# Keys ahead of queries, value scaling in halves on ScalarE, a shorter scale chain and a new order in a fused attention and mixture-of-experts kernel

## The chip, the cores and the metric

The kernel runs on one core of a Trainium2 chip. The metric is the device time of one execution in microseconds (us); a kernel's time is the median of several runs. The core has TensorE (PE, matrix products into the accumulator memory PSUM; PEld is its weight load), VectorE (DVE), ScalarE (ACT), GpSimd (POOL) and SyncE (SP), which here issues the transfers.

## The reference

```python
# attention: batch 4 x 8 heads, 768 tokens, head size 48
k_n = k / (np.linalg.norm(k, axis=-1, keepdims=True) + 1e-06)
for t in range(S):
    y[:, :, t] = np.einsum('bhd,bhde->bhe', q[:, :, t], state)
    v_old = np.einsum('bhde,bhd->bhe', state, kt)
    state = state + bt[:, :, :, None] * np.einsum('bhd,bhe->bhde', kt, vt - v_old)
# mixture of experts: 4 x 768 tokens of 384, 8 experts of width 1024
for s in range(S):
    fresh_e = int(np.argmax(logits[b, s]))
    e = fresh_e if s == 0 or local_gate[b, s] < 0.5 else prev_e
    ...
    out[b, s] = p[e] * (np.maximum(x[b, s] @ w1[e], 0.0) @ w2[e])
```

The attention output y is the input x of the experts. The state depends on the token before, so the kernel works in chunks of tokens: inside a chunk a triangular system replaces the steps one by one.

## The kernel before

**Chunks and macros.** 768 tokens are 12 chunks n of 64 tokens (all 32 heads at once); two chunks make one macro m = n // 2. For a chunk, `K(n)` loads its keys and queries (two tiles `W`, 512 KB each), takes the products of keys with keys and with queries (the Gram matrix, 48 matmuls per tile) into PSUM, and copies three parts out: the key products within each 32 tokens into `gt` (ACT L199 writes it, DVE L204 adds its other part), the cross part into `G2` (ACT L201), the query products under a mask into `am` (DVE L202). `T_(m)` transposes `gt` into L (DVE L212, two halves), and makes the scales: sum of squares `ss` (L214), its root (ACT L215), then seven small DVE operations (L216, L218, L220), the start value (`Diag`, L225) and the scaled system L (L226, L227). nT (L222) holds the key norms by which values are scaled.

**The solve.** Each macro's triangular system is solved in steps of two instructions. Macro 0 uses blocks of 16 (15 steps, L244 and L245), the others blocks of 32 (31 steps, L240 and L241). Macro 2 runs on DVE in PSUM, the other five on POOL; they are called S0, S1, S3, S4, S5 here. A macro's solution X is transposed (L253, L256), and `Tc(n)` builds from it the chunk's operand `XT`.

**Values and state.** Each chunk's values arrive in `kv` (768 KB); L313 multiplies them by nT, on DVE for eight chunks and POOL for four. `online(n)` then carries the state: matmuls fk and fq (keys and queries with the state), R (L325), p1 with XT, Us (ACT L339), the new state (ACT L346), p2, and the output y of the chunk (ACT L352, DVE L353). Below, O6 is this part for chunk 6 and U6 the query and y part of it. y goes to HBM (xs) and comes back transposed for the routing products (L362, L365).

**Experts.** After ten chunks a first share of tokens is routed, gathered and run through the experts while the last chunks still work; the rest follows.

**What sets the order.** All operations are numbered when the program is built, and the string ORDER lists the numbers with an engine letter (S, P, V, A, G, I). Every engine executes its operations in that order and waits in front of one whose inputs or buffers aren't ready. Buffers come from pools: 14 `W` tiles, three `kv`, three PSUM accumulators `pr`, two `gt`. An operation that may run on one of several engines (L313: `e='VG'`) runs on the one that ORDER names.

Of the kernel before, what the change touches and what calls it, by code (L numbers as in the profile page):

```python
# [70 lines left out]
class Attn:  # L71
# [4 lines left out]
    ORDER='''11S 7G 199S 8G 12S 24S 25S 79S 0G 2G 14P 9G 19P 15A 16A 18V 17V 26P 22V 21A 31P 67S 27A 29V 13S 20A 66S 30V 32A 4S 23V 99A 80S 35V 181S 36V 37V 74P  # L76
38V 39A 44A 40V 41V 28A 76A 69P 42V 75A 68S 45V 46V 153S 211S 77V 47G 198S 71A 43V 48G 210S 70A 78V 197S 72V 81P 49G 73V 50G 34V 10V 86P 51G 82A 83A
52G 85V 87A 53G 84V 88A 33A 90V 54G 92V 55G 91V 56G 89V 217P 182V 93V 57G 94A 212P 220V 219A 218A 154G 3V 221V 205P 213A 58G 95V 96V 59G 200P 97V 207A
60G 1A 215V 448S 206A 61G 280S 202A 216V 322S 214A 100V 101V 5S 201A 63V 103G 104G 62V 105G 64V 138P 106G 209V 107G 208V 139A 65V 108G 204V 140P 109G
223V 110G 222V 102V 111G 203V 224V 225A 230A 226V 112G 98V 227V 166P 281G 228V 142V 324S 113G 141V 231V 167A 233V 147A 168P 232V 114G 234V 235V 236V  # L80
115G 6V 237V 116G 238V 144P 169V 117G 239V 240V 145A 118G 170V 146P 241V 119G 172P 151A 150A 242V 149A 243V 152A 120G 148A 143A 244V 171A 155P 121G
245V 178A 173A 246V 175A 122G 174P 156A 247V 355A 157P 123G 248V 179A 249V 176A 159P 124G 306S 177A 323S 180A 250V 158A 125G 251V 183P 160A 252V 126G
229V 161V 127G 253V 185P 163S 128G 184V 336S 129G 254V 186P 335S 130G 255V 256V 131G 187A 257V 132G 190P 133G 258V 134V 188P 191A 135V 164P 404S 300A
165V 270A 192V 330P 136V 193S 342P 331A 194S 332A 334V 303A 333V 343A 405G 345V 344A 337P 296A 346V 274A 137V 325P 307G 338A 340V 326A 341V 339A 328V
327A 271P 329V 272A 195P 347V 277A 273P 189A 348V 349V 196V 350A 279A 351V 297P 276A 352V 275A 298A 353V 278A 299P 572S 357V 162S 356V 282P 358V 304A
301A 359G 259V 305A 302A 360G 260V 284P 283V 361G 362G 261V 262V 285P 446S 363G 263V 447S 264V 364G 286A 479A 287P 365G 289P 265A 430S 366G 288A 267V
367G 290A 308P 291V 368G 449P 354V 293S 309V 369G 310P 266V 570S 269V 370G 311P 460S 452V 584S 371G 312A 394A 315P 372G 401A 313P 316A 431V 294P 451A
373G 268V 420A 450A 317V 459S 374G 528S 295V 454P 319S 453V 375G 466P 455A 424A 458V 457V 398A 376G 461P 469V 456A 467A 377G 395P 378G 462A 396A 529V
468A 397P 427A 379G 470V 314A 465V 471V 421P 402A 380G 399A 403A 472V 463A 381G 473V 464V 474A 422A 400A 475V 320P 382G 423P 321V 476V 383G 406P 425A
428A 477V 384G 429A 480V 482V 408P 385G 407V 481V 409P 571S 386G 292S 387G 410A 388G 411P 389G 483G 390V 413P 652S 412A 583S 484G 426A 391V 414A 432P  # L90
485G 393V 548A 486G 392V 487G 415V 519P 488G 433V 417S 434P 520A 489G 518A 490G 435P 668S 491G 318S 521P 436A 492G 493G 437P 523A 522A 418P 554S 524A
# [905 lines left out]
```

## Time and the profile before

| | |
|---|---|
| three runs | 486.12, 486.02, 483.58 us; median 486.02 us |
| profiled execution | 483.22 us, of which the profile's span is 481.4 us |
| busy share of the span | PE 80%, DVE 69%, POOL 54%, ACT 39% |

The profile's execution has 1.8 us around its span. Times inside the trace count from the span's start. A row of a timeline gives start, length, engine, line, operation, output and inputs, and in brackets how long the engine was idle before and what ended that. A busy share is a mean over stages with different limits, so the rows that count are those of the stage in question.

### The profile page before, as it was taken

The numbers are of one execution on the slowest core, as the hardware profiler recorded it, in microseconds if no ns is written. First come the engines' busy times: TensorE is split into PE (matmuls) and PEld (weight loads), VectorE is DVE, ScalarE is ACT, GpSimd is POOL, SyncE is SP. The second block draws the span as 40 slices with busy tenths as digits, with TensorE's granted clock in tenths as the row PEclk, the third lists the DMA queues.
The fourth block names the chain that finished last, engine by engine and source line by source line (L and its number), as shares of the span: only waits on it lengthen the run. The fifth ranks groups of instructions, "written<-read, shape, count | busy, mean of one in ns | idle before, by whom it ended". The sixth has DMA issues, their size and how long they took to land. (4 is left out here: it accounts for less than half of the span.)

```text
span 481.4 us, 20215 instructions
## 1 busy us (share of the span) xinstructions
PE 383.2 (80%) x8907; PEld 291.6 (61%) x8907; DVE 333.3 (69%) x705; ACT 189.9 (39%) x340; POOL 260.7 (54%) x438
## 2 busy tenths in 40 slices
PE   5545676676775657685869999999999999999994
PEld 4535575575775656574658768675655656566662
DVE  1999877846661848689426878578787995958551
ACT  2531263643635354633645204225234251625120
POOL 5388881288878858986512353864251424351301
PEclk9795557777689777557679999999999999999999
DMA  8632037458165656518533235767665657585301
GB/s 294 258 132 98 4 114 204 68 177 275 39 199 170 127 156 154 157 35 210 189 101 76 59 106 180 163 130 260 183 203 145 192 180 226 160 269 163 92 1 48
DMA packets 61691, 72.19 MB, mean 150 GB/s; under 512 B 40172, under 2 KB 51534, under 8 KB 61600
## 3 DMA queue, kind: packets, MB, share of 16 engines
q1 hardware_dynamic: 58048, 60.90, 44.4%
q0 software_dynamic: 3552, 9.96, 6.3%
q8 instruction: 71, 1.16, 1.0%
q14 instruction: 20, 0.16, 0.1%
HBM read 52.53 MB, written 9.95 MB: 130 GB/s over the span
## 5 line engine op out<-in xcount | busy, mean ns | idle before, releaser
L241 POOL TENSOR_TENSOR X<-X,fg 128x31 f32<-128x31 f32 (+15 forms) x124 | 74.3, 600 | 9.7
L240 POOL TENSOR_TENSOR fg<-L,X 128x31 f32<-128x31 f32 (+15 forms) x124 | 64.9, 523 | 24.3 <-DVE X L225 8.3
L487 DVE TENSOR_SCALAR gf<-pr 128x384 f32<-128x384 f32 (+5 forms) x68 | 33.5, 495 | 26.5 <-PE pr L485 12.7
L154 PE MATMUL pr<-W 64*64 64x64 f32 (+1 forms) x1152 | 34.4, 281 | 21.7 <-DMA W<-in_kq_dram 7.6
L154 PE MATMUL pr<-S,W 64*64 64x48 f32 x1408 | 37.5, 274 | 14.6 <-issue 10.5
L154 PEld LDWEIGHTS pr<-S,W 64*64 64x64 f32 x1408 | 34.7, 189 | 19.1 <-issue 13.4
L154 PEld LDWEIGHTS pr<-W 64*64 64x64 f32 x1152 | 31.6, 168 | 24.1 <-issue 9.1
L485 PE MATMUL pr<-kv,xtp 128*128 128x384 f16 (+3 forms) x186 | 43.7, 298 | 0.8 <-ACT W L486 0.8
L492 PEld LDWEIGHTS <-W 128*128 128x128 f16 x288 | 27.7, 98 | 19.1 <-POOL W L699 1.4
L485 PEld LDWEIGHTS <-W 128*128 128x128 f16 x288 | 27.8, 99 | 17.6 <-issue 0.7
L485 PE MATMUL pr<-kv,W 128*128 128x448 f16 (+2 forms) x144 | 37.8, 341 | 0.0
L486 ACT ACTIVATE L<-pr 128x384 f16<-128x384 f32 (+3 forms) x34 | 15.2, 447 | 53.7 <-PE pr L485 23.6
L475 POOL DMA_INDIRECT out_dram<-y,so x9 | 11.2, 1249 | 45.8 <-DVE y L502 44.9
L485 PE MATMUL pr<-kv,amp 128*128 128x448 f16 (+3 forms) x120 | 34.4, 311 | 0.0
L486 ACT ACTIVATE W<-pr 128x256 f16<-128x256 f32 (+4 forms) x34 | 14.8, 441 | 46.0 <-PE pr L485 40.4
L473 POOL DMA_INDIRECT G<-xs,gi x23 | 26.0, 1129 | 7.0 <-issue 6.4
L470 DVE SCALAR_TENSOR_TENSOR W<-W,W 128x768 f16<-128x768 f32 (+1 forms) x23 | 26.3, 1143 | 3.2 <-ACT W L468 3.2
L154 PE MATMUL pr<-Us,amp 64*64 64x48 f32 x768 | 18.8, 251 | 12.0 <-issue 8.7
L492 PE MATMUL pr<-amp,L 128*128 128x384 f16 x116 | 28.3, 326 | 0.0
L492 PEld LDWEIGHTS <-L 128*128 128x128 f16 (+1 forms) x208 | 20.7, 101 | 12.2 <-issue 0.2
L492 PE MATMUL pr<-W,W 128*128 128x384 f16 x156 | 27.2, 326 | 0.0
L485 PEld LDWEIGHTS <-xtp 128*128 128x128 f16 x216 | 21.1, 98 | 9.5
(364 smaller groups left out, 979.5 us busy)
## 6 DMA issues: line engine op xcount, KB each, us to landing
W<-in_kq_dram SPq DMA_DIRECT2D x24, 512.0 KB, 5.5
W<-in_moe_w_dram SPq DMA_DIRECT2D x30, 384.0 KB, 3.4
W<-in_moe_w_dram SPq DMA_DIRECT2D x22, 512.0 KB, 4.4
kv<-in_kv_dram SPq DMA_DIRECT2D x12, 768.0 KB, 4.7
...
amp<-in_moe_w_dram SPq DMA_DIRECT2D x2, 512.0 KB, 6.7
...
```

Of the source, the lines that this page charges most:

```text
L154: mm=lambda o,l,r,st,sp,tp:MM(o,l,r,start=st,stop=sp,skip_group_check=True,tile_position=tp)
L240: eng.tensor_tensor(tv,l[:,j,j+1:].unsqueeze(2).to_broadcast([128,n,k]),x[:,j,0:k].unsqueeze(1).to_broadcast([128,n,k]),op=ALU.mult)
L241: eng.tensor_tensor(x[:,j+1:,0:k],x[:,j+1:,0:k],tv,op=ALU.subtract)
L470: def wlo(s,st,w,k): s.nc.vector.scalar_tensor_tensor(s.wv(w,k)[:,1],s.wst(st,k),256.0,s.wv(w,k)[:,0],op0=ALU.mult,op1=ALU.subtract)
L473: return s.nc.gpsimd.indirect_dma_start(out=x[0:m],out_offset=None,in_=s.xs[0:nt,:],in_offset=bass.IndirectOffsetOnAxis(ap=ix[0:m],axis=0) ...
L475: I=s.nc.gpsimd.indirect_dma_start(out=s.out[:,:],out_offset=bass.IndirectOffsetOnAxis(ap=ix[0:m],axis=0),in_=y[0:m],in_offset=None,bounds ...
L485: for k in range(3): s.nc.tensor.matmul(ps,s.wv(W[k],k)[:,a,0,128*f:128*f+128],xT[:,3*b+k,:],start=(x==0 and k==0),stop=(x==2 and k==2))
L486: def uphi(s,h,ps): s.nc.scalar.activation(h,ps,AF.Relu,scale=2.0**-6)
L487: def upt(s,t,ps): s.nc.vector.tensor_scalar(t,ps,0.0,2.0**-6,op0=ALU.max,op1=ALU.mult)
L492: s.nc.tensor.matmul(po[0:m],h(a,f)[:,c:c+m],s.wv(W[k],k)[:,b,f%2,:],start=(x==0 and f==0),stop=(x==2 and f==7))
```

## The change

1. For chunks 0 and 1 the host stores each key-and-query tile with the keys first. The program loads the key half of a tile (128x512) in one transfer and the query half in another, and forms the Gram products in two halves of 16 matmuls: the key half feeds `gt` and `G2`, the query half `am`. Each half takes a PSUM accumulator of its own.
2. The value scaling of a chunk is two operations of eight heads each, 24 in all. ORDER puts 21 on ACT (eight 128x48 instructions each, the scale a column of nT), two on POOL and one on DVE.
3. The addition of the other part into `gt` may run on ACT, as two copies of 32 partitions. ORDER does so for 10 of the 24 tiles.
4. The scale chain: behind the root stand three DVE operations in front of the scaled L; nT and what leads to it are operations of their own. L is scaled in a part of 8 columns and one of 24 (before two of 16), and a solve of blocks of 32 waits for the first part only until its eighth step.
5. ORDER is another order of all operations (1133 against 1107).

The experts' code, the pools' sizes and the engine of each solve stay.

```diff
-    ORDER='''11S 7G 199S 8G 12S 24S 25S 79S 0G 2G 14P 9G 19P 15A 16A 18V 17V 26P 22V 21A 31P 67S 27A 29V 13S 20A 66S 30V 32A 4S 23V 99A 80S 35V 181S 36V 37V 74P
...
+    ORDER='''11S 2G 12S 28S 29S 7G 109A 14P 8G 17S 53A 24S 30P 13S 15A 40S 9G 16A 20V 5S 21P 32A 33S 31A 210S 18P 36V 22A 25P 19V 76S 75S 27V 37P 88S 26V 89S 38A
...
+                if n<2:
+                    add(lambda g=g:nc.sync.dma_start(KQ[g].t.rearrange("r a t -> r (a t)")[:,0:512],s.kq_[n,g][:,0:512]),w=[(KQ[g],0)],claim=[KQ[g]],e='S',c=262144); s.kl[n]=S.ops[-1]
...
+                def fh(z,ps,g=g):
+                    k=KV(KQ[g].t,n)
+                    for u in range(4):
+                        for j,c,q in H:
+                            w=0 if u%2==0 else 1-z; y,d=q^w,c^w; mm(ps.t[B(y),d,128*u+64*z:128*u+64*z+64],k[B(j),u,q,0,:],k[B(j),u,q,z,:],u==0,True,(64*j,64*y))
...
+                def gh(e,go=go,gv=gv):
+                    if e is nc.vector: e.scalar_tensor_tensor(go(),gv()[:,:,:,32:64],s.ma[:,1:2],go(),op0=ALU.mult,op1=ALU.add)
+                    else:
+                        for q in range(2): o=slice(64*q+32,64*q+64); e.copy(go()[o],gv()[o,:,:,32:64])
...
-                add(lambda go=go,gv=gv:nc.vector.scalar_tensor_tensor(go(),gv()[:,:,:,32:64],s.ma[:,1:2],go(),op0=ALU.mult,op1=ALU.add),r=[ps,"mask",key],p=[gt],claim=[gt],c=485)
+                add(gh,r=[ps0,"mask",key],p=[gt],claim=[gt],e='VA',c=dict(V=485,A=760))
...
-            def f2():
-                nc.vector.tensor_mul(t0.t,t0.t,ss.t); nc.vector.tensor_add(t0.t,t0.t,s0.t); nc.vector.tensor_scalar(nn.t,t0.t,0.5,1e-6,op0=ALU.mult,op1=ALU.add); nc.vector.reciprocal(mu.t,nn.t)
...
-            def f3(): nc.vector.tensor_mul(t0.t,mu.t,b.t); nc.vector.tensor_mul(mu.t,mu.t,t0.t)
...
+            add(lambda:nc.vector.tensor_scalar_add(nn.t,ss.t,1e-12),r=[ss],w=[(nn,0)],claim=[nn],c=190)
...
+            def f2(): nc.vector.scalar_tensor_tensor(mu.t,s0.t,2e-6,nn.t,op0=ALU.mult,op1=ALU.add); nc.vector.reciprocal(mu.t,mu.t); nc.vector.tensor_mul(mu.t,mu.t,b.t)
...
-                add(fm,r=[(L,j//16)],w=[(Z,0),("fm",E_)],claim=[L,Z],e=EE,c=520+3.8*ne if EE=='G' else 400+2.15*ne); S.ops[-1].lock=not ps
+                add(fm,r=[(L,j//8 and 1)],w=[(Z,0),("fm",E_)],claim=[L,Z],e=EE,c=520+3.8*ne if EE=='G' else 400+2.15*ne); S.ops[-1].lock=not ps
...
-            add(lambda e:e.tensor_tensor(v(),v(),nT.t[:,16*cc:16*cc+16].unsqueeze(2).to_broadcast([128,16,48]),op=ALU.mult),r=[nT],w=[(kv,1)],claim=[kv],e='VG',c=dict(V=1050,G=1550)); S.ops[-1].pre.add(S.ops[-2]); S.ops[-1].lock=1
...
+            for h in range(2):
+                def sv(e,h=h):
+                    a=v()[:,8*h:8*h+8]; t=16*cc+8*h
+                    if e is nc.scalar:
+                        for x in range(8): e.mul(a[:,x],a[:,x],nT.t[:,t+x:t+x+1])
+                    else: e.tensor_tensor(a,a,nT.t[:,t:t+8].unsqueeze(2).to_broadcast([128,8,48]),op=ALU.mult)
```

**The first transfers.** SP's queue at the start of the program, before; W0 and W1 are the tiles of chunk 0, W2 and W3 those of chunk 1, bt the betas.

```order
L182 DMA W0_77<-in_kq_dram 128x1024
L185 DMA bt0_103<-in_beta_dram 128x32
L182 DMA W1_78<-in_kq_dram 128x1024
L182 DMA W2_79<-in_kq_dram 128x1024
L182 DMA W3_80<-in_kq_dram 128x1024
L182 DMA W4_81<-in_kq_dram 128x1024
```

The same place now:

```order
L185 DMA W0_77<-in_kq_dram 128x512
L185 DMA W1_78<-in_kq_dram 128x512
L185 DMA W2_79<-in_kq_dram 128x512
L185 DMA W3_80<-in_kq_dram 128x512
L217 DMA W0_77<-in_kq_dram 128x512
L217 DMA W1_78<-in_kq_dram 128x512
L189 DMA bt0_103<-in_beta_dram 128x32
L217 DMA W3_80<-in_kq_dram 128x512
```

The four key halves now stand ahead of every query half.

**The first scale chain.** DVE's queue from the transpose of `gt` to the scaled system of macro 0, before; s00 is the root, mm0 the scale, X1 the solution's tile.

```order
L212 STREAM_TRANSPOSE L0_120<-gt_112 128x512 x2
L214 TENSOR_SCALAR ss0_109<-L0_120 128x32
L216 RECIPROCAL t00_111<-s00_110 128x32
L218 TENSOR_TENSOR t00_111<-t00_111,ss0_109 128x32
L218 TENSOR_TENSOR t00_111<-t00_111,s00_110 128x32
L218 TENSOR_SCALAR nn0_105<-t00_111 128x32
L218 RECIPROCAL mm0_108<-nn0_105 128x32
L220 TENSOR_TENSOR t00_111<-mm0_108,bt1_104 128x32
L220 TENSOR_TENSOR mm0_108<-mm0_108,t00_111 128x32
L225 COPY X1_123<-mm0_108 128x32
L227 TENSOR_TENSOR L0_120<-L0_120,mm0_108 128x2x16x16
```

The same place now:

```order
L231 STREAM_TRANSPOSE L0_120<-gt_112 128x512 x2
L233 TENSOR_SCALAR ss0_109<-L0_120 128x32
L234 TENSOR_SCALAR nn0_105<-ss0_109 128x32
L236 SCALAR_TENSOR_TENSOR mm0_108<-s00_110,nn0_105 128x32
L236 RECIPROCAL mm0_108<-mm0_108 128x32
L236 TENSOR_TENSOR mm0_108<-mm0_108,bt0_103 128x32
L247 TENSOR_TENSOR L0_120<-L0_120,mm0_108 128x2x16x16
L245 COPY X1_123<-mm0_108 128x32
```

Seven operations between root and scaling became three, and the start value moved behind the scaling.

**ScalarE around the first operands.** ACT's queue before, where chunk 0's operand xtp0 is built and chunk 0 and 1 leave PSUM (QQ0, Q10: copies of products; Us0: L339).

```order
L267 COPY Q10_129<-pr1_148 128x512
L307 COPY xtp0_97<-TT0_124 32x16x32
L295 COPY QQ0_130<-pr0_147 128x256
L308 ACTIVATE xtp0_97<-pr0_147 32x2x4x32
L307 COPY xtp0_97<-TT0_124 32x16x32
L308 ACTIVATE xtp0_97<-pr0_147 32x2x4x32 x3
```

The same place now:

```order
L338 ACTIVATE kv2_102<-kv2_102,nT1_107 128x48 x8
L338 ACTIVATE kv1_101<-kv1_101,nT0_106 128x48 x8
L315 COPY QQ0_130<-pr0_147 128x256
L287 COPY Q10_129<-pr2_149 128x512
L328 ACTIVATE xtp0_97<-pr0_147 32x2x4x32 x3
L306 ACTIVATE xtp0_97<-TT0_124,ma_76 128x16x32
L327 COPY xtp0_97<-TT0_124 32x16x32
L338 ACTIVATE kv2_102<-kv2_102,nT1_107 128x48 x8
```

Groups of eight value scalings now stand between the copies that empty PSUM.

## Rows read from the trace of the kernel before

**Rows 1.** Page, busy time of engines: us, share of the span, instructions.

```profile
PE 383.2 (80%) x8907; PEld 291.6 (61%) x8907; DVE 333.3 (69%) x705; ACT 189.9 (39%) x340; POOL 260.7 (54%) x438
```

**Rows 2.** Windows: length, busy us of PE, PEld, DVE, ACT, POOL; PE clock; DMA share; GB/s.

```profile
35.37:74.30 38.93, 24.59 (x1185) 22.91 (x1186) 34.49 (x78) 13.22 (x24) 34.21 (x63) 0.51 0.25 78
...
95.75:134.40 38.65, 27.78 (x1216) 25.73 (x1211) 23.24 (x49) 18.15 (x36) 33.85 (x62) 0.72 0.50 157
...
179.20:222.50 43.30, 30.74 (x1209) 28.62 (x1210) 35.03 (x76) 19.36 (x31) 38.47 (x62) 0.65 0.54 144
...
265.00:481.40 216.40, 207.98 (x1646) 131.89 (x1643) 154.59 (x323) 69.31 (x116) 82.24 (x76) 1.00 0.53 153
```

**Rows 3.** POOL's waits: waited for, us in total, times, longest.

```profile
POOL fg L244 <- DVE L L227: 10.5, 1, 10.5
```

**Rows 4.** POOL's timeline: the starts of S1, S3 and S4.

```profile
35.37 0.24 POOL L240 TENSOR_TENSOR fg<-L,X 128x31 f32<-128x31 f32 x1 [0.69 <-DVE L L226]
...
95.75 0.51 POOL L240 TENSOR_TENSOR fg<-L,X 128x31 f32<-128x31 f32 x1 [8.29 <-DVE X L225]
...
135.75 0.24 POOL L240 TENSOR_TENSOR fg<-L,X 128x31 f32<-128x31 f32 x1 [1.37 <-DVE L L226]
```

**Rows 5.** POOL's timeline: start of S5, first gather behind S5.

```profile
179.20 0.24 POOL L240 TENSOR_TENSOR fg<-L,X 128x31 f32<-128x31 f32 x1 [4.58 <-ACT xtp L308]
...
225.18 1.27 POOL L473 DMA_INDIRECT hz<-xs,gi  x1 [2.73 <-DVE gi L669]
```

**Rows 6.** PE's timeline at the start.

```profile
4.20 1.98 PE L154 MATMUL pr<-W 64*64 64x128 f32 x48 [4.20 <-DMA W<-in_kq_dram]
7.85 5.04 PE L154 MATMUL pr<-W 64*64 64x128 f32 x144 [1.67 <-DMA W<-in_kq_dram]
```

**Rows 7.** Transfers of 0 to 8 us: packets, bytes, rate.

```profile
DMA packets 653, 1.90 MB, mean 237 GB/s; under 512 B 194, under 2 KB 194, under 8 KB 653
```

**Rows 8.** Transfer issued first: KB, us to landing.

```profile
W<-in_kq_dram SPq DMA_DIRECT2D x1, 512.0 KB, 3.3
```

**Rows 9.** ACT's timeline at the start.

```profile
6.30 1.28 ACT L199 ACT_TABLE_LOAD   x1 [6.30 <-PE pr L154]
...
12.97 0.47 ACT L199 ACTIVATE gt<-pr,ma 128x256 f32<-128x256 f32 x1 [0.52 <-PE pr L154]
```

**Rows 10.** DVE's timeline at the start.

```profile
14.02 1.99 DVE L212 STREAM_TRANSPOSE L<-gt 128x512 f32<-128x512 f32 x2
...
16.53 0.35 DVE L216 RECIPROCAL t<-s 128x32 f32<-128x32 f32 x1 [0.29 <-ACT s L215]
...
18.58 0.68 DVE L227 TENSOR_TENSOR L<-L,mm 128x512 f32<-128x512 f32 x1
```

**Rows 11.** Groups of ACT by shape: xcount, busy us, mean ns, idle before.

```profile
L308 ACT ACTIVATE xtp<-pr 32x256 f32<-32x256 f32 x48 | 17.3, 372 | 10.7 <-PE pr L154 10.2
...
L215 ACT ACTIVATE s<-ss 128x32 f32<-128x32 f32 x6 | 1.4, 230 | 11.6 <-DVE ss L214 11.5
```

**Rows 12.** Groups of DVE by shape, the same columns.

```profile
L204 DVE SCALAR_TENSOR_TENSOR gt<-pr,ma,gt 128x256 f32<-128x256 f32 x8 | 3.6, 478 | 13.9 <-ACT G L201 9.9 <-ACT gt L199 3.9
```

**Rows 13.** Line L313, value scaling: duration ns minimum/median/maximum.

```profile
L313 DVE TENSOR_TENSOR kv<-kv,nT x8: 895/950/1373, 28.0 to 238.5; 128x768 f32<-128x768 f32 x8
...
L313 POOL TENSOR_TENSOR kv<-kv,nT x4: 1472/1474/1477, 30.1 to 86.0; 128x768 f32<-128x768 f32 x4
```

**Rows 14.** DVE's timeline from S0's end to S3's start.

```profile
35.15 1.90 DVE L253 STREAM_TRANSPOSE TT<-X 128x512 f32<-128x512 f32 x2
```

**Rows 15.** PE's timeline in the same stretch.

```profile
74.13 1.21 PE L154 MATMUL pr<-S,W 64*64 64x48 f32 x36 [1.99 <-issue]
```

**Rows 16.** DVE's timeline ahead of S5.

```profile
176.75 0.96 DVE L353 SCALAR_TENSOR_TENSOR y<-pr,y 128x768 f16<-128x768 f32 x1 [5.09 <-ACT y L352]
177.70 1.23 DVE L470 SCALAR_TENSOR_TENSOR W<-W,W 128x1024 f16<-128x1024 f32 x1
...
178.93 0.17 DVE L365 TENSOR_SCALAR lg<-pr 128x18 f32<-128x18 f32 x1
```

More of the change, by code (lines that the diff above doesn't have):

```diff
@@ L79 @@
[L79 to L82, printed above, removed]
@@ L225, in T_, with fL @@
             add(lambda e:e.tensor_copy(zt()[:,0:1024:33],mu.t),r=[mu],w=[(Z,0),(Z,1)],claim=[Z],e='V',c=300)
-            def fL(e,z): l=full(L.t)[:,16*z:16*z+16]; e.tensor_mul(l,l,mu.t.unsqueeze(1).to_broadcast([128,16,32]))
+            def fL(e,z): a,b_=((0,8),(8,32))[z]; l=full(L.t)[:,a:b_]; e.tensor_mul(l,l,mu.t.unsqueeze(1).to_broadcast([128,b_-a,32]))
             def fl(e): l=blk(L.t); e.tensor_mul(l,l,mu.t.rearrange("p (z b) -> p z b",z=2).unsqueeze(2).to_broadcast([128,2,16,16]))
             if Bk==32:
-                for z in range(2): add(lambda e,z=z:fL(e,z),r=[mu,ss],w=[(L,z)],claim=[L],e='V',c=670); S.ops[-1].lock=1
+                for y in range(2): add(lambda e,z=y:fL(e,z),r=[mu,ss],w=[(L,y)],claim=[L],e='V',c=(400,1030)[y]); S.ops[-1].lock=1
             else: add(fl,r=[mu,ss],w=[(L,0),(L,1)],claim=[L],e='V',c=670); S.ops[-1].lock=1
             if ps:
-                for o in S.ops[i1-8-s.TS:]: o.boost=12e4
+                for o in S.ops[i1-9-s.TS:]: o.boost=12e4
             S.tag=('S',m)
@@ L323, in fk @@
                         for j,c,q in H: y,d=q^u%2,c^u%2; mm(pk.t[B(y),d,e48(u)],k(j,q,u,0),S0.t[B(j),q,u,:],u==0,True,(64*j,64*y))
[L324 to L325 removed]
+                add(fk,r=[*KQ,*((x,z) for x in KQ for z in range(2)),S0],w=[pk],e='P',c=1500); S.ops[-1].pc=(1800,1130,3.07,64); S.ops[-1].pre.update(C['xt']); ok=S.ops[-1]
+                add(lambda:nc.vector.tensor_tensor(R.t,kv.t[:,1].rearrange("p (c x) -> p c x",c=2),pk.t[:,:,0:384],op=ALU.subtract),r=[pk,(kv,1,0),(kv,1,1)],w=[R],claim=[kv],c=cv(768)+40)
                 S.tag=('U',n)
@@ L329, in fq @@
                         for j,c,q in H: mm(py.t[B(c),j,e48(u)],k(j,q,u,1),S0.t[B(j),q,u,:],u==0,False,(64*j,64*c))
-                add(fq,r=[*KQ,S0],w=[py],e='P',c=1500); S.ops[-1].pc=(1800,1130,3.07,64); S.ops[-1].pre.update([ok]+([ch[n-3]['lf']] if n>2 else [])); oq=S.ops[-1]; S.tag=('O',n)
-                rv=lambda q,c,u:R.t[B(q),c,e48(u)]; Rk=R
-            else: rv=lambda q,c,u:kv.t[B(q),1,384*c+48*u:384*c+48*u+48]; Rk=(kv,1)
+                add(fq,r=[*KQ,*((x,z) for x in KQ for z in range(2)),S0],w=[py],e='P',c=1500); S.ops[-1].pc=(1800,1130,3.07,64); S.ops[-1].pre.update([ok]+([ch[n-3]['lf']] if n>2 else [])); oq=S.ops[-1]; S.tag=('O',n)
+                rv=lambda q,c,u:R.t[B(q),c,e48(u)]; Rk=[R]
+            else: rv=lambda q,c,u:kv.t[B(q),1,384*c+48*u:384*c+48*u+48]; Rk=[(kv,1,0),(kv,1,1)]
             def p1():
```

109 lines of the change are left out of this document (62 added, 47 removed).

## The prediction, made before the changed kernel was run

> **What bounds the kernel now.** I read the page's busy shares first, then the windows by stage, then POOL's waits and timeline, then the timelines of the engines that POOL waits for. The busy shares [rows 1] name TensorE, but they are a mean. In the windows [rows 2] PE is dense only behind 265 us: 207.98 of 216.40 us, at a granted clock of 1.00. Before that no engine is full. So the end is the moment at which the dense part begins, plus some 216 us that the change does not touch; what the change is worth is how much earlier the attention gets there.
>
> Ahead of it the work is a relay. POOL solves S0, S1, S3, S4, S5 one after another, and its waits and timeline show the places where the relay stands still. It begins S0 at 19.45 (the edge of my first window; it waited 10.5 us for the scaled L [rows 3]), S1 at 35.37 after 0.69, S3 at 95.75 after a long gap, S4 at 135.75 after 1.37 [rows 4], S5 at 179.20 after 4.58 [rows 5]. So three starts carry the sum: S0 (limited by loads and a DVE chain), S3 (DVE and PE, while DVE also solves macro 2) and S5 (the chain of state and outputs).
>
> **The head.** Before, PE does the first tile's 48 matmuls at 4.20 (1.98 us) and then waits for a transfer until 7.85; the other 144 take 5.04 [rows 6]. By 8 us 1.90 MB have moved, 237 GB/s over the window [rows 7], and one 512 KB load issued into an empty queue takes 3.3 us to land [rows 8]. Four full tiles are 2.1 MB; the four key halves are half of that. At the same mean they are in by 8/1.9 × 1.05 = 4.4 us; by issue, since PE's first start at 4.20 puts the first issue at about 0.9, and with 1.3 us that I allow for three more, by 2.2 + 3.3 = 5.5. I take 5.3. A half is 16 matmuls, 0.6 us by the row of 144. It needs a third accumulator's release by one `am` or `gt` (0.5 to 0.7 each), so I put the last key half at 7.4 to 8.1. Its `gt` costs 0.47 on ACT [rows 9] and 0.48 on DVE [rows 12], or two copies of 0.37 on ACT [rows 11]. ACT's first table load, 1.28 us, stands on the path at 6.30 [rows 9]; in the new order it stands with two zero fills ahead of the first product, where ACT has nothing to do until about 4.9. So `gt` is full at about 9.5 and the DVE transposes begin at 9.6 instead of 14.02 [rows 10]. Bounds: 8.3 if ACT never waits (behind 4.9 stand four `gt` of 0.47, two `G2` and two copies of 0.37: 3.4 us), 11.5 if the fourth half queues behind a query half.
>
> The chain behind: the transposes take 1.99, the root comes back 0.52 after them (16.53 against 16.01), then seven operations take 2.05 up to L227 at 18.58, L227 0.68 [rows 10]. Three operations of 0.35, 0.2 and 0.2 are 0.8 with their pitches. So from 9.6: +2.0 +0.5 +0.8 +0.7 +0.2 for the start value behind it +0.2 to POOL = 14.0. I add 0.6 for waits that I can't see: **S0 at 14.6, 4.85 earlier** (3 to 6). S0 itself sheds the 1.47 scaling that stood inside it [rows 13]; the two-instruction steps stay. S0's end: 4.85 + 1.47 = 6.3 earlier.
>
> **From S0 to S3.** DVE begins S0's transposes at 35.15; S3 starts at 95.75 [rows 4, 14]. The 60.6 us between are a chain through DVE (macro 2's scale chain and its solve, the outputs) and PE (the state's products of chunk 1, still at 74.13 [rows 15], and then the Gram products of chunks 6 and 7). In it the change removes four DVE operations from macro 2's chain and four from macro 3's, 1.2 us each by the head's count, and moves three `gt` additions of 0.48 off DVE [rows 12]: 2.4 + 1.4 = 3.8. It adds on ACT five scaling halves and three pairs of copies.
>
> The price of a scaling half isn't in the trace: eight ACT instructions of 128x48. The nearest rows are 230 ns for 128x32 and 372 for 32x256 [rows 11], so 1.84 to 2.98 us a half; I take 1.95, near the first since 48 columns are near 32. DVE paid 0.95/2, POOL 1.474/2 a half [rows 13]. So 21 halves put 41 us on ACT, and ten pairs of copies 7.4: 190 us become 238 of some 470, half of the span. The rows leave the room: in the stretch from 35.37 ACT is 13.2 of 38.9 busy, in S3's 18.15 of 38.65 [rows 2].
>
> The Trainium skill, "ScalarE: Activation LUTs", section "Rules for kernel authors", says to do multiplications on VectorE and not on ScalarE, and so speaks against this part; from the instruction costs of the same page (186 ns + 0.833 ns an element, 93 more for the scale operand, overlapping by 93) I get an estimate of 1.9 us a half, so its sum would be the same. What would follow from it as an outcome is the rival of a late ACT below.
>
> Some halves stand ahead of copies that empty PSUM. Of five halves I count half a half each on average as 1.0 us in all on the path (0 if each falls into ACT's idle time, 9.8 if all are on it). So S3: 6.3 + 3.8 − 1.0 = **9.1 earlier, at 86.6** (85 to 90). PE's stall of 1.99 that nothing in the profile explains [rows 15] may move or vanish; I leave it.
>
> **S3 to S5.** S3 and S4 keep their steps. The wait of 1.37 ahead of S4 [rows 4] shrinks, since the solve starts when 8 columns of L are scaled: up to 1.2 back, but S4's end isn't what S5 waits for. S5 waits for its start value, which stands on DVE behind U6's output: that began at 176.75 after 5.09 us of waiting for ACT, then a weight conversion of 1.23 stood between [rows 16]. The trace names ACT xtp as S5's releaser, but nothing in S5's first step reads xtp, and the start value stands between the rows of 177.70 and 178.93; I take that. In the new order the conversion is gone from between, and two routing operations (0.18 each) and the small part of L (0.35) stand there: 0.5 less. The U6 chain begins in S3's stretch and shifts with it; six halves and one pair of copies (12.5 us) join ACT there, 18.15 + 12.5 of 38.65 = 79%. The four chunks' scalings gone from DVE return 0.95 each where DVE was in demand; I set that against ACT's delays. **S5 9.6 earlier.** S5 took 43.3 us, S3 38.65 for the same 62 instructions [rows 2]; less DVE work beside it may return up to 1 us. Behind S5, POOL now converts weights ahead of the gathers (which stood at 225.18 [rows 5]), and PE takes chunks 10 and 11 ahead of the first expert: between −4 and +2, for which I put 0.3 of loss against the 1 us.
>
> **Sum.** 9.6 + 1 − 0.3 = 10.3. The profiled execution took 483.22, of which 1.8 lies around the span: 472.9. The median of the three runs is 2.8 above it: 475.7. I say 474.0, between them; alone, this case has 470 to 479.
>
> **Rivals.**
>
> *ACT is late, no faster or slower.* ACT works in order; between S3's start and U6 stand nine halves, 17.6 us by my price, 26.8 by the upper one. Each that stands ahead of a copy of the state or of Us with PE waiting lengthens the chain to S5 by its whole 1.95. At 5 of 9 on the path, 10 us, the gain is gone (483 to 486); at all nine 490. For it: 79% in S3's stretch, and PE idles there often. Against it: PE's and ACT's idle times alternate in these stretches, and a half has a whole chunk's time, some 20 us, before R needs it. Chance 0.18, of which 0.11 is slower by over 0.5%.
>
> *Only the head gains.* S3 could be held by something not moved, as the key load of chunk 7 or the stall on PE, so that S1 and S2 move and S3 by the head alone, and part is lost again before S5: 5 us, 479 to 481. For it: the long gap ahead of S3 while POOL idles; against it: the gap's releasers are all DVE and PE operations that shift with S0. Chance 0.10.
>
> *The halves land no sooner.* If a load's time is mostly fixed and all share the same engines, the last key half lands with the bulk behind it, at about 7.5: the head gains only its chain and the table load, 2 us less than I say for S0 and for all that follows, and more if the query halves crowd in: 477 to 481. By rows: one load alone took 3.3 us for 512 KB, which at the later rate would be a good part fixed. Chance 0.05. The Trainium skill, "DMA: Bandwidth & Descriptors", section "Rules for kernel authors", wants 1 MiB a transfer, and would point to this; the trace has no 256 KB load to test it.
>
> *More.* If S5's wait of 4.58 falls with the chain (U6's output was late by the wait for ACT, 5.09) and the tail keeps its interleaving, 4 to 6 us more: 465 to 470. Chance 0.17.
>
> **Chances and range.** The forecast has 0.50. About 0.5% is what a measurement of this kernel can tell from no change. Faster by more: 0.50 + 0.17 + 0.10 + 0.05 = 0.82; within it 0.07 and slower 0.11, both from a late ACT. The range goes from 465 to 482; it leaves out the late ACT and a little of the low end. What I can't price is PE's clock: 0.51 in the stretch from 35.37 against 0.72 and 1.00 later [rows 2], near its lower level of 1.2 GHz; another spacing of matmuls may change it.
>
> **What would show it.** S0 starts at 14 to 15.5 with the transposes at 9 to 10.5; a scaling half is 1.8 to 2.1 us on ACT; S3 starts at 85 to 88; S5 at 168 to 171; behind 265 less about 10 PE is as dense as before. Wrong: transposes behind 12 (loads or accumulators); S3 behind 90 with DVE waiting for ACT (scaling in the way); U6's output later than 83 us after S3's start.

## The result and the profile after

The changed kernel is slower: 490.4 us against 485.0 on the same chip (20 runs each), ratio 1.0142 [1.0103, 1.0180]. Two more comparisons, in later groups of runs, gave 1.0102 [1.0033, 1.0172] and 1.0079 [1.0047, 1.0111]. A group of runs stands on one chip, and the groups differ (in six of them the kernel before had medians from 481.7 to 494.1 us). So a ratio is always to the kernel before on the same chip, and kernels are compared within a group where they can be. Two profiles of one kernel differ by up to 6 us at a stage, too: a single stage time says little, the same sign in several profiles says something. 474.0 us (465 to 482) had been predicted.

The page of the changed kernel, busy time of each engine, answers to [rows 1]; the profiled execution took 491.16 us, its span 489.4.

```profile
PE 388.2 (79%) x8971; PEld 297.2 (61%) x8971; DVE 323.4 (66%) x688; ACT 235.6 (48%) x532; POOL 260.2 (53%) x440
```

DVE lost 9.9 us and ACT gained 45.7, as planned. PE gained 5.0 of busy time and 64 matmuls.

POOL's timeline of the changed kernel: the starts of S0, S3, S4 and S5 and the first gather (L500).

```profile
19.79 0.24 POOL L264 TENSOR_TENSOR fg<-L,X 128x30 f32<-128x30 f32 x1 [10.87 <-DVE X L245]
...
95.45 0.24 POOL L260 TENSOR_TENSOR fg<-L,X 128x31 f32<-128x31 f32 x1 [23.65 <-DVE L L246]
...
138.93 0.24 POOL L260 TENSOR_TENSOR fg<-L,X 128x31 f32<-128x31 f32 x1 [6.19 <-DVE X L245]
...
180.01 1.04 POOL L260 TENSOR_TENSOR fg<-L,X 128x31 f32<-128x31 f32 x1 [3.68 <-DVE X L245]
...
228.79 1.47 POOL L544 TENSOR_TENSOR W<-W,c 128x768 f32<-128x768 f32 x1 [8.10 <-ACT W L495]
230.34 1.66 POOL L544 TENSOR_TENSOR W<-W,W 128x768 f16<-128x768 f32 x1
231.94 0.83 POOL L339 TENSOR_TENSOR kv<-kv,nT 128x384 f32<-128x384 f32 x1
233.29 1.26 POOL L500 DMA_INDIRECT hz<-xs,gi  x1 [0.51 <-DVE tq L698]
```

Against [rows 3 to 5]: S0 0.3 later, S3 0.3 earlier, S4 3.2 later, S5 0.8 later, the first gather 8.1 later, the end of the span 8.0 later. In this profile none of the three starts that carry the sum came more than 0.3 earlier; S1, at 33.19, was 2.2 earlier, and that was gone by S3. Two later profiles of the changed kernel, from other groups, have S0 at 19.64 and 20.13, S3 at 93.31 and 94.38 and S5 at 176.76 and 175.85. There S5 is 2.4 and 3.4 earlier than in the profile of before, and the kernel is slower all the same (1.0102 and 1.0079).

**The head.** PE's timeline at the start, against [rows 6], then DVE's, against [rows 10]:

```profile
4.45 1.13 PE L156 MATMUL pr<-W 64*64 64x64 f32 x32 [4.45 <-DMA W<-in_kq_dram]
5.87 1.98 PE L156 MATMUL pr<-W 64*64 64x64 f32 x64 [0.28 <-DMA W<-in_kq_dram]
8.55 3.80 PE L156 MATMUL pr<-W 64*64 64x64 f32 x125 [0.70 <-DMA W<-in_kq_dram]
14.46 0.33 PE L156 MATMUL pr<-W 64*64 64x64 f32 x3 [2.10 <-issue]
```

```profile
14.82 0.69 DVE L221 TENSOR_TENSOR amp<-pr,mask 128x512 f32<-128x512 f32 x1 [3.40 <-PE pr L156]
15.43 1.99 DVE L231 STREAM_TRANSPOSE L<-gt 128x512 f32<-128x512 f32 x2
...
17.96 0.19 DVE L236 SCALAR_TENSOR_TENSOR mm<-s,nn 128x32 f32<-128x32 f32 x1
18.19 0.35 DVE L236 RECIPROCAL mm<-mm 128x32 f32<-128x32 f32 x1
18.58 0.19 DVE L236 TENSOR_TENSOR mm<-mm,bt 128x32 f32<-128x32 f32 x1
18.80 0.69 DVE L247 TENSOR_TENSOR L<-L,mm 128x512 f32<-128x512 f32 x1
```

A half is 32 matmuls in the trace and takes 1.13 us. The text ahead of the prediction says 16: that is the program's count, and a product of f32 operands leaves two matmuls here; two halves are 64 where a whole tile was 48. The products of halves run on to 14.79 on PE. Three key halves are done at 7.85; then PE waits until 8.55 for a query half, and the last key half stands behind two query halves (its products take from 10.49 to 11.62). So `gt` was full at 12.94. On DVE an `am` (L221, which writes amp) stands ahead of the transposes and waited 3.40 us for a query half, 2.10 of it a stall of PE that the profile calls "issue" (no wait that it shows). The transposes begin at 15.43 instead of 14.02. The short chain behind them is as costed: 0.84 from 17.96 to 18.80, where before took 2.05. These 1.2 us are all that the head gained, and the 1.4 of later transposes gave them back.

**Behind S5.** From S5's start to the end of chunk 9's output (the last DVE operation on its y) the changed kernel took 48.2 us, and the kernel before 43.3. This difference is in every profile of this document: 47.0 to 52.6 us in the 12 with the new order in this stretch, 42.5 to 44.1 in seven of the eight with the old one (47.1 in the eighth, which has all scalings on ACT). Part of it is work moved forward: PE has 1406 matmuls there instead of 1205, and from there to chunk 11's output the changed kernel took 1.4 us less. But PE's stalls without a named wait come to some 10 us in this stretch instead of 5.9, and it waits for chunk outputs on their way back from HBM (xt). Before, its only wait for xt, 2.08 us at 227.47, stands behind chunk 9's output. PE's row after:

```profile
202.84 0.47 PE L389 MATMUL pr<-wc,xt 128*128 128x18 f16 x12 [3.03 <-DMA xt<-y]
```

PE's waits from chunk 11's output to the end, before (263 us on) and after (267.4 on), and the windows of these stretches (the columns of [rows 2]):

```profile
PE Sps L492 <- POOL W L699: 1.0, 1, 1.0
PE pr L485 <- ACT W L486: 0.8, 1, 0.8
```

```profile
PE pr L508 <- DMA Us<-xs,gi: 2.4, 1, 2.4
PE pr L512 <- DVE gf L514: 1.3, 2, 0.8
PE pr L838 <- DVE gf L514: 1.2, 1, 1.2
```

```profile
263.00:481.40 218.40, 209.98 (x1663) 133.58 (x1660) 155.60 (x326) 70.08 (x118) 84.17 (x77) 1.00 0.53 153
```

```profile
267.40:489.40 222.00, 210.03 (x1666) 133.70 (x1664) 159.05 (x323) 71.19 (x120) 85.10 (x78) 0.99 0.54 150
```

From chunk 11's output to the end the kernel took 218.4 us before and 222.0 after, with PE busy for 210.0 in both: the 3.6 are idle time. The gather of the second share of tokens (Us) lands late, and its products wait 2.4 us (2.9 and 3.4 in the two later profiles of the changed kernel).

### The profile page after: what moved, and what is told of

Same layout as the page of the kernel before. It is cut to its first block, busy times and chain, and to the rows that moved or that the text cites. A ratio compares the mean times of both kernels' runs of the same rounds, so it can differ in the third digit from the quotient of the medians.

```text
span 489.4 us, 20533 instructions
## 1 busy us (share of the span) xinstructions
PE 388.2 (79%) x8971; PEld 297.2 (61%) x8971; DVE 323.4 (66%) x688; ACT 235.6 (48%) x532; POOL 260.2 (53%) x440
## 3 DMA queue, kind: packets, MB, share of 16 engines
q1 hardware_dynamic: 58624, 60.90, 44.1%
## 5 line engine op out<-in xcount | busy, mean ns | idle before, releaser
L261 POOL TENSOR_TENSOR X<-X,fg 128x31 f32<-128x31 f32 (+15 forms) x124 | 69.6, 561 | 9.7
L156 PE MATMUL pr<-W 64*64 64x64 f32 (+1 forms) x1216 | 37.8, 296 | 17.4 <-DMA W<-in_kq_dram 9.2
L512 PE MATMUL pr<-kv,W 128*128 128x448 f16 (+3 forms) x240 | 49.6, 312 | 1.3 <-DVE gf L514 1.3
L156 PEld LDWEIGHTS pr<-W 64*64 64x64 f32 x1216 | 35.1, 185 | 19.6 <-DMA W<-in_kq_dram 4.9
L512 PE MATMUL pr<-kv,amp 128*128 128x384 f16 (+4 forms) x156 | 43.9, 317 | 0.0
L338 ACT ACTIVATE kv<-kv,nT 128x48 f32<-128x48 f32 x168 | 39.8, 322 | 4.6 <-DMA kv<-in_kv_dram 4.5
L512 PEld LDWEIGHTS <-amp 128*128 128x128 f16 x240 | 23.6, 98 | 13.7 <-issue 1.7
L500 POOL DMA_INDIRECT G<-xs,gi x23 | 25.8, 1123 | 7.0 <-issue 6.4
L519 PE MATMUL pr<-W,L 128*128 128x384 f16 x116 | 28.3, 326 | 0.0
L495 ACT ACTIVATE W<-W 128x768 f16<-128x768 f32 (+1 forms) x27 | 24.7, 924 | 6.1 <-DMA W<-in_moe_w_dram 4.2
L380 DVE SCALAR_TENSOR_TENSOR y<-pr,y 128x768 f16<-128x768 f32 x12 | 11.4, 953 | 23.1 <-ACT y L379 23.0
```

Source lines behind the costliest of these rows:

```text
L156: mm=lambda o,l,r,st,sp,tp:MM(o,l,r,start=st,stop=sp,skip_group_check=True,tile_position=tp)
L261: eng.tensor_tensor(x[:,j+1:,0:k],x[:,j+1:,0:k],tv,op=ALU.subtract)
L338: for x in range(8): e.mul(a[:,x],a[:,x],nT.t[:,t+x:t+x+1])
L380: add(lambda:nc.vector.scalar_tensor_tensor(y.t[:,:,1,:],py.t[:,:,0:384],256.0,y.t[:,:,0,:],op0=ALU.mult,op1=ALU.subtract),r=[py,(y,0)],w= ...
L495: if e in (None,s.nc.scalar): s.nc.scalar.mul(o,i,256.0)
L500: return s.nc.gpsimd.indirect_dma_start(out=x[0:m],out_offset=None,in_=s.xs[0:nt,:],in_offset=bass.IndirectOffsetOnAxis(ap=ix[0:m],axis=0) ...
```

## Experiments

**The head's order.** One edit of ORDER: all four key halves' products first, the `am` operations behind the transposes. PE's queue, program products:

```diff
 L156 MATMUL pr_149<-W_78 64x64 x16
-L156 MATMUL pr_147<-W_77 64x64 x16
-L156 MATMUL pr_148<-W_78 64x64 x16
 L156 MATMUL pr_147<-W_80 64x64 x16
-L156 MATMUL pr_148<-W_79 64x64 x16
+L156 MATMUL pr_148<-W_77 64x64 x16
+L156 MATMUL pr_149<-W_78 64x64 x16
+L156 MATMUL pr_147<-W_79 64x64 x16
```

> The changed kernel with one piece of its order rewritten: the fourth key half's products stand ahead of every query half on TensorE, and the query halves' masked copies stand behind the first transposes on VectorE. Theory C (the head lost its gain because the fourth key half queued behind two query halves and because VectorE waited 3.4 us for a query half ahead of its transposes): transposes start at 10.5 to 12 instead of 15.43, S0 at 15 to 16.5 instead of 19.79, S1 3 us earlier; if what follows is a chain, the whole kernel gets 3 to 4 us faster, about 1.006 of the time before. Theories A and B: S0 starts earlier too, but the gain is lost again before S5, 1.012 to 1.016.

Measured: 0.9965 [0.9923, 1.0007]. On another chip again:

> The second experiment's kernel again, beside the others of this call on one chip. It gave 0.9965 on the slowest of the chips so far, and with the scaling on VectorE 1.0102 on another. If its gain is its own: 0.993 to 1.000. If it was the chip: 1.004 to 1.012.

0.9998 [0.9959, 1.0037]. S0 starts at 15.03 and 15.11 in these two, within the predicted 14 to 15.5. But on these chips the changed kernel itself had not run, so one more group of four kernels went onto one chip, with the changed kernel, this one, and both with the scalings on DVE:

> The changed kernel again, as the corner of a table of two by two on one chip. All theories expect what it showed twice: 1.010 to 1.014 of the kernel before.

> The changed kernel with the repaired head, on the same chip. If the repair is what gave 0.9965 and 0.9998 on two other chips, it is 1.0 to 1.5% below the changed kernel here too; if those were differences between chips, less than 0.5%.

Changed 1.0079 [1.0047, 1.0111], repaired head 1.0050 [1.0017, 1.0084]: 0.3% apart, intervals overlapping. That is what one chip shows of the repair; the larger differences above are between runs on different chips, and may be the chips' own. With both profiles from one chip one sees where the 4.2 us at S0 go.

The first part goes on DVE. With the repair S0's last step ends 4.4 us earlier (29.05 and 33.49), but S0's transposes (L273) begin only 2.5 earlier: DVE comes to them without a wait, because macro 1's scales and the copies of later Gram products stand ahead of them in its order. In the pair with the scalings on DVE (below) they are 3.2 earlier (30.17 and 33.41). The row of the changed kernel, then that with the repaired head:

```profile
33.53 1.96 DVE L273 STREAM_TRANSPOSE TT<-X 128x512 f32<-128x512 f32 x2 [0.39 <-POOL X L265]
```

```profile
31.00 1.96 DVE L273 STREAM_TRANSPOSE TT<-X 128x512 f32<-128x512 f32 x2
```

The rest goes on PE's way to S3. PE's and DVE's timelines of the changed kernel in this group: chunk 6's first products; U1's output (L380) and the transposes of macro 3 ahead of S3.

```profile
82.64 1.83 PE L156 MATMUL pr<-W 64*64 64x128 f32 x48 [0.17 <-DVE y L380]
```

```profile
81.63 0.96 DVE L380 SCALAR_TENSOR_TENSOR y<-pr,y 128x768 f16<-128x768 f32 x1 [2.44 <-ACT y L379]
...
89.81 1.99 DVE L231 STREAM_TRANSPOSE L<-gf 128x512 f32<-128x512 f32 x2
```

The same with the repaired head, S0's start on POOL, then PE, then DVE:

```profile
15.96 0.24 POOL L264 TENSOR_TENSOR fg<-L,X 128x30 f32<-128x30 f32 x1 [7.04 <-DVE X L245]
```

```profile
73.00 1.20 PE L156 MATMUL pr<-R,xtp 64*64 64x48 f32 x40 [2.65 <-issue]
...
80.91 0.88 PE L156 MATMUL pr<-W 64*64 64x128 f32 x27 [0.34 <-DVE y L380]
83.17 2.43 PE L156 MATMUL pr<-W 64*64 64x128 f32 x69 [1.38 <-issue]
```

```profile
79.90 0.96 DVE L380 SCALAR_TENSOR_TENSOR y<-pr,y 128x768 f16<-128x768 f32 x1 [1.34 <-ACT y L379]
...
89.42 2.00 DVE L231 STREAM_TRANSPOSE L<-gf 128x512 f32<-128x512 f32 x2
```

S0 begins at 20.13 without and 15.96 with the repair, S3 at 94.38 and 93.49, S5 at 175.85 and 176.25; the spans are 487.3 and 487.7. Macro 3's key products stand behind U1's output, which is 1.7 earlier and gives them an accumulator; U1 is on PE's chain of state products. Stalls of PE stand in both places in the repaired kernel (2.65 ahead of U1, 1.38 in the key products), where the changed one has 1.90 and none, and 0.9 us is left at S3. The pair with the scalings on DVE (below) behaves otherwise: 4.1 earlier at S0 (19.42 and 15.37), 3.7 at S3, 3.8 at S5, and then 0.9 at chunk 9's output and 0.3 at the span's end, its medians 3.3 us apart. POOL's S3 and S5 there, without and with the repair:

```profile
96.04 0.24 POOL L260 TENSOR_TENSOR fg<-L,X 128x31 f32<-128x31 f32 x1 [23.53 <-DVE L L246]
...
180.12 1.04 POOL L260 TENSOR_TENSOR fg<-L,X 128x31 f32<-128x31 f32 x1 [3.93 <-DVE X L245]
```

```profile
92.38 0.24 POOL L260 TENSOR_TENSOR fg<-L,X 128x31 f32<-128x31 f32 x1 [22.92 <-DVE L L246]
...
176.32 1.04 POOL L260 TENSOR_TENSOR fg<-L,X 128x31 f32<-128x31 f32 x1 [3.93 <-DVE X L245]
```

So the early start is carried as far as S5 in one of two cases, and lost by the end of the profile in both.

**The same head in the order of before.** Keys first, everything behind the head as before:

```diff
-    ORDER='''11S 7G 199S 8G 12S 24S 25S 79S 0G 2G 14P 9G 19P 15A 16A 18V 17V 26P 22V 21A 31P 67S 27A 29V 13S 20A 66S 30V 32A 4S 23V 99A 80S 35V 181S 36V 37V 74P
+    ORDER='''11S 2G 12S 28S 29S 7G 107A 14P 8G 17S 52A 24S 30P 13S 15A 40S 9G 16A 20V 21P 32A 33S 31A 87S 37P 36V 22A 38A 27V 43V 18P 23A 39A 25P 34P 75S 74S 88S
...
+                if n<2: add(lambda fh=fh,ps=ps:fh(0,ps),r=[(KQ[g],0)],w=[ps],claim=[gt,G2],e='P',c=1500); S.ops[-1].pc=(1100,650,1.2,16)
```

> The kernel before with the keys-first head alone, with all four key halves ahead of the query halves; behind the head its old order, its old scale chain, and the scalings where they were. S0 starts at 15.5 to 16.5 (4 less than 19.45, with the old chain of seven operations). By the prediction's relay model everything behind shifts by 3 to 4 us: 0.991 to 0.995. If a gain at the start is lost in waits and in stalls of TensorE's instruction stream before the dense part: 0.997 to 1.005.

Measured 1.0024 [0.9984, 1.0064]. Its POOL timeline, S3 and S5:

```profile
93.84 0.50 POOL L258 TENSOR_TENSOR fg<-L,X 128x31 f32<-128x31 f32 x1 [8.42 <-DVE X L243]
...
182.07 0.24 POOL L258 TENSOR_TENSOR fg<-L,X 128x31 f32<-128x31 f32 x1 [7.01 <-ACT xtp L326]
```

S0's start (15.75) and S3's (93.84) were 3.7 and 1.9 earlier than in the profile of before (from another chip), and S5's 2.9 later. Here, too, the first part goes on DVE: S0's last step ends at 30.82, and its transposes begin at 33.58 without a wait before them. In the old order an early S0 was worth nothing that could be measured.

**Value scaling.** On ACT in the order of before, all 24 halves:

```diff
-            add(lambda e:e.tensor_tensor(v(),v(),nT.t[:,16*cc:16*cc+16].unsqueeze(2).to_broadcast([128,16,48]),op=ALU.mult),r=[nT],w=[(kv,1)],claim=[kv],e='VG',c=dict(V=1050,G=1550)); S.ops[-1].pre.add(S.ops[-2]); S.ops[-1].lock=1
+                    if e is nc.scalar:
+                        for x in range(8): e.mul(a[:,x],a[:,x],nT.t[:,t+x:t+x+1])
...
+                add(sv,r=[nT],w=[(kv,1,h)],claim=[kv],e='VGA',c=dict(V=520,G=770,A=2200)); S.ops[-1].pre.add(dk); S.ops[-1].lock=1
```

> The kernel before in its old order, with one part of the change alone: each value scaling in two halves of eight ScalarE instructions at the place where VectorE or GpSimd did it (all 24 halves, 46 us on ScalarE, of which 40 were added in the changed kernel too). Theory A: 1.010 to 1.025, with R and the copies of Us and of the state waiting behind scalings. Theory B: 0.995 to 1.005, since ScalarE is 40% busy and the scalings fall into its idle time.

Measured 1.0162 [1.0092, 1.0232]. PE's waits between 35 and 222 us, which name ACT:

```profile
PE pr L155 <- ACT xtp L309: 7.7, 2, 5.7
PE pr L155 <- ACT QQ L296: 6.7, 5, 2.7
PE pr L155 <- ACT G L202: 4.4, 1, 4.4
```

In the same stretch these three were 2.9, 2.0 and 1.2 us before. That is the late ACT of the first rival, in an order that doesn't know of the halves. In the changed kernel's order it is not so: there QQ is 4.0 and G 0.3. With the 21 halves put back on DVE (ORDER's letters alone, 193A to 193V and so on):

> The changed kernel in its new order, but the 21 scaling halves that were on ScalarE (8 instructions of 128x48 each) run on VectorE at the same places. Theory A (ScalarE is late: scaling halves in front of the copies that empty PSUM hold the chain of state and outputs up): ScalarE loses 40 us of work, the outputs of chunks 1 to 9 come 4 to 8 us earlier than in the changed kernel, and the time falls from 1.014 of the time before to about 1.00 or below (480 to 486 us). Theory B (the new order as such, with where TensorE's instruction stalls fall and what stands ahead of the first gathers, costs the time): 1.010 to 1.020, since VectorE takes over 21 x 0.76 = 16 us and nothing else moves. Theory C (only the head's lost gain matters): 1.010 to 1.016.

1.0072 [1.0030, 1.0114], on a chip where the changed kernel wasn't timed; and together with the repaired head:

> The changed kernel with both edits of the first two experiments: the fourth key half ahead of the query halves, and the 21 scaling halves on VectorE. If the two losses are of different places and add (0.018 of the head, 0.007 of the scaling): 0.987 to 0.992. If the later start only buys waiting elsewhere: 0.994 to 1.000.

1.0102 [1.0063, 1.0141], beside the changed kernel on that chip:

> The changed kernel unchanged, beside the others of this call on one chip: 1.010 to 1.018 of the time before by every theory. If it is below 1.008 here, what the second experiment gained on the changed kernel is smaller than the two ratios from different chips say.

1.0102. The table on one chip settles it:

> The changed kernel with the scaling halves on VectorE, beside the changed kernel on one chip. If scaling on ScalarE costs by itself: 0.5% or more below the changed kernel. If it helps: 0.5% or more above. If it depends on the head: below here, and above in the pair with the repaired head.

> Repaired head and scaling halves on VectorE, on the same chip. If the effects add: as far from the repaired head as the second kernel is from the changed one. If they interact, as the runs on different chips suggest: 1.0% above the repaired head, while the second kernel is below the changed one.

1.0187 [1.0132, 1.0242] against the changed kernel's 1.0079: scaling on DVE is 1.1% slower. With the repaired head 1.0104 [1.0050, 1.0158] against 1.0050, 0.5% slower, intervals overlapping. The pairs that other groups hold agree: on DVE without the repair against on ACT with it, 1.1% there and 1.4% here; changed kernel against repair and DVE, 0.0 and 0.2%. So ACT is the better place in this order, and not what made the change slow; the 1.0072, set against other chips, had suggested the opposite. The group of the changed kernel by shape, which answers to [rows 13]:

```profile
L338 ACT ACTIVATE kv<-kv,nT 128x48 f32<-128x48 f32 x168 | 39.8, 322 | 4.6 <-DMA kv<-in_kv_dram 4.5
```

39.8 us over 21 halves are 1.9 each. The Trainium skill, "ScalarE: Activation LUTs", "Rules for kernel authors", wants multiplications on VectorE: the order of before bears that out (1.0162), the changed order doesn't (1.0187 on DVE against 1.0079).

**The chain alone.** The short chain and the parts of 8 and 24 columns in the order of before:

```diff
-            def f3(): nc.vector.tensor_mul(t0.t,mu.t,b.t); nc.vector.tensor_mul(mu.t,mu.t,t0.t)
...
+            def f2(): nc.vector.scalar_tensor_tensor(mu.t,s0.t,2e-6,nn.t,op0=ALU.mult,op1=ALU.add); nc.vector.reciprocal(mu.t,mu.t); nc.vector.tensor_mul(mu.t,mu.t,b.t)
```

> The kernel before in its old order, with the short scale chain and the split of L (8 and 24 columns) alone. By the prediction's steps S0 starts 1.0 us earlier, S3 2 to 3 us earlier, the whole 2 to 4 us faster: 0.992 to 0.997. Theory A says the same, since nothing of this is on ScalarE but one small operation. Theory B (a gain at a solve's start is swallowed by stalls and waits further on): 0.997 to 1.003.

Measured 1.0065 [1.0028, 1.0101], with S0 at 18.04, 1.4 earlier than in the profile of before (from another chip): again an early start that gives nothing.

**The order behind chunk 9's output.** ORDER spliced there: new order's end on the kernel before; old order's end on the changed kernel, and on the one with the repaired head. POOL's queue around the gathers, in the second:

```diff
-L544 TENSOR_TENSOR W_86<-W_86,c_170 128x768
-L544 TENSOR_TENSOR W_78<-W_86,W_78 128x768
-L339 TENSOR_TENSOR kv_102<-kv_102,nT_107 128x384
 L500 DMA hz_131<-xs,gi 128x768
```

> The kernel before, its code and its order up to chunk 9's output, and behind that the changed kernel's order. Theory B: 3 to 6 us slower, 1.006 to 1.013, all of it behind chunk 9's output. Else 0.998 to 1.003.

> The changed kernel up to chunk 9's output in its new order, and everything behind that in the order of before (chunks 10 and 11, the second routing, all expert work; the gathers ahead of the weight conversions on GpSimd, the first expert's products interleaved with chunks 10 and 11 on TensorE). Theory B (the new order costs behind chunk 11's output: there the changed kernel took 222 to 224 us to the end, the old order 218.2 to 218.4): that stretch falls back to 218 to 219 and the ratio from 1.010 to 1.014 to about 1.000 to 1.004. If the loss is the scaling or the head and the tail only looks longer, because work slips into it: 1.008 to 1.014.

> The changed kernel with the repaired head of the second experiment and the old tail of the ninth. If both losses are of their own: 0.985 to 0.995, faster than both kernels. If the gain at the start is used up before chunk 9's output, as in the seventh experiment: 0.997 to 1.004.

On one chip, with the repaired head's 0.9998: new end alone 1.0137 [1.0082, 1.0193], old end on the changed front 1.0051 [1.0011, 1.0092], old end with repaired head 0.9988 [0.9960, 1.0017]. With the old end the wait for the gather is gone and from chunk 11's output to the end it takes 224.4 and 223.6 us, with the new end 226.6 and 226.9. But with the new front, chunks 10 and 11 come later under the old end (43.4 and 43.9 us from chunk 9's output to chunk 11's, against 39.1), so the sum is the same. The new end is bad on the old front. Behind the new front, with the repaired head, the exchange changes nothing that could be measured (0.9998 and 0.9988): what the new end gains for chunk 11 it gives back behind it.

**A mere shift.** Idle products that nothing reads, in the order of before, ahead of chunk 0's first 32-row products:

```diff
+                if n==0:
+                    for x in range(32): mm(s.Sps[0:64,0,448:464],s.mask[0:64,0:64],s.mask[0:64,0:16],True,True,(0,0))
```

> The kernel before with 32 idle products (64 matmuls in the trace, about 2 us, in a wait of TensorE ahead of 37.2 us, into an unused corner of an accumulator) and nothing else. It moves every later instruction of TensorE by 64 places. In the trace TensorE stands still for 0.5 to 3.7 us at every 128th pair of weight load and matmul while the small matmuls run close together; this moves those stalls to other operations. If the place of the stalls counts (a stall on the chain of the state costs its length, elsewhere nothing): a difference of 1 to 4 us either way, 0.992 to 1.008 but not 1, and the stalls stand 64 pairs from where they stood. If it doesn't: 0.998 to 1.002.

Measured 1.0097 [1.0058, 1.0136]. Then with 64 and with 16 products (128 and 32 matmuls):

> The kernel before with 128 idle matmuls ahead of 37 us (64 gave 1.0097). If it counts where the stalls fall, 128 puts them back on the products on which they fell before, one stall more: 1.000 to 1.005, less than with 64. If the matmuls' own work costs: twice that of 64, about 1.02.

> The kernel before with 32 idle matmuls there. If the matmuls' own work costs: half of 64, about 1.005. If it counts where the stalls fall: anything from 0.995 to 1.012, not in proportion to the number.

1.0124 [1.0082, 1.0166] and 0.9978 [0.9952, 1.0005]. PE's timelines there with 64 matmuls, and with 128:

```profile
32.51 4.88 PE L154 MATMUL Sps<-mask 64*64 64x16 f32 x64
37.32 1.93 PE L154 MATMUL pr<-TT,gt 32*32 32x32 f32 x128
```

```profile
32.31 8.91 PE L154 MATMUL Sps<-mask 64*64 64x16 f32 x128
41.15 1.93 PE L154 MATMUL pr<-TT,gt 32*32 32x32 f32 x128
```

Before, the product after them began at 37.20 after 4.71 us of idle time. 64 fit into that (0.1 later), 128 don't (4.0 later), which spoils the second as a test: most of its 1.24% may be that delay. What stands is that 64 matmuls without visible delay cost 1.0% on one chip, and 32 nothing on another. Neither profile names a cause. What I see to differ is where PE's stalls fall (with 64 the longest is 4.4 us, at 126.42, before 3.7); that this is the cause is not shown.

## Why the prediction was wrong

*The step that failed* is the first, that ahead of 265 us "the work is a relay" in which POOL's starts carry the sum, and with it the term of 0.3 us of loss behind S5. The profiled execution ended 18.3 us behind the forecast one; 10.4 of them had arisen by S5's start and 7.9 arose behind it. The relay first: S0 was brought to about its predicted start in both orders, and of some 4 us 0.9 to 3.7 were left at S3, 3.8 or less than nothing at S5; the medians gained nothing in the old order (1.0024) and 1.3 or 3.3 us in the new. S0's transposes wait for their turn on DVE; S3 hangs on U1's output as well as on S0's end, and so on PE's chain of state products; S5's start decides little, since chunk 9's output and the gathers are PE's chain again. I had left PE's stalls out as something that "may move or vanish". They add up to 39.7 us before and to 39.6, 43.0 and 46.4 in three profiles of the changed kernel, and to 32.6 in the slowest kernel of all (scaling on ACT in the old order), so their sum doesn't make the difference; those that fall on that chain do lengthen it. PE's rows from S5's start in the first profile, where before has 2.15 and 0.35:

```profile
180.33 1.51 PE L156 MATMUL Sps<-Us,kv 64*48 64x48 f32 x58 [3.51 <-issue]
184.76 3.54 PE L156 MATMUL pr<-S,W 64*64 64x48 f32 x122 [1.53 <-issue]
190.68 1.62 PE L156 MATMUL pr<-R,xtp 64*64 64x48 f32 x50 [2.12 <-issue]
```

*S0 4.85 earlier*: 0.3 later. I had all four key halves in by 5.3. Three landed at 4.41, 5.05 and 5.82; the fourth's landing is not in that trace, and in the seven other profiles that have it, it came at 6.2 to 8.1. So the rival of halves that land no sooner (7.5) came true in part, but it didn't decide: the order held the fourth half's products back to 10.49 anyway, and with the order repaired S0 starts at 14.6 to 16.0. The term was mis-sized by the half's 0.6 us (it takes 1.1) and lost through the query halves, my own upper bound ("if the fourth half queues behind a query half") exceeded: 15.43 against 11.5.

*S0's start to S3's, 4.25 shorter* (1.47 and 2.8): 75.7 us against 76.3, 0.6 shorter (74.2 and 73.7 in the two later profiles), although the chain has its predicted 0.8 and DVE is relieved. *A scaling half 1.95 us*: right, 1.9. *Late ACT*: not the cause; scaling on DVE is slower. U6's output, the sign that I named, ended 83.7, 82.6 and 80.6 us after S3's start in the three profiles (82.0 before). *S5 one us shorter*: 40.7 us against 43.3, more than that. *Behind S5, 0.3 of loss*: S5's end was 1.8 earlier and the span's 8.0 later, so about 10 were lost. About 6 of them lie ahead of chunk 11's output and 3.6 behind it. One group shows the loss on one chip, without the profile of before but with two kernels that have its order behind the head (the same head in the order of before, and the shift by 64). There S5 began at 182.07 and 180.96 in these and at 176.76 in the changed kernel; chunk 11's output ended at 262.0 and 264.4, and at 261.2; the span at 480.3 and 482.6, and at 485.2. So the changed kernel was ahead at S5 and at chunk 11's output and behind at the end. The windows from that output to the end, of the shift by 64 and of the changed kernel:

```profile
264.38:482.60 218.22, 209.94 (x1662) 133.55 (x1660) 155.67 (x325) 70.09 (x118) 84.15 (x77) 1.00 0.53 153
```

```profile
261.16:485.20 224.04, 211.58 (x1666) 134.49 (x1664) 159.01 (x323) 71.19 (x120) 85.10 (x78) 0.99 0.53 149
```

The dense part, which I took as fixed, has 4.2 us more idle and 1.6 more busy time there, 2.9 of the idle time in the wait for the gather. In the other two groups with profiles of both ends the new end is longer by 1.0 to 4.6 us, whatever stands ahead of it. From group to group this stretch differs as much with one and the same old end (218.2 to 224.9), so it is compared within a group alone.

*What stays open.* The change's ratio (1.008 to 1.014) isn't the sum of its parts: the short chain alone is 1.0065, the head alone 1.0024, the scaling alone 1.0162, the new end alone 1.0137, and the whole with another head order is 0.9965 to 1.0050. A shift of 64 matmuls alone made 1.0% on the one chip where it ran. How much of the loss belongs to such placement and how much to the order's waits can't be told from these runs. No version was clearly faster than before. The lowest ratios of a changed order are the repaired head's 0.9965 [0.9923, 1.0007], with 0.9998 and 1.0050 on other chips, and 0.9988 [0.9960, 1.0017] for it with the old end.
